# Two LN2 outputs and an exponential later on ScalarE, one Wo product later on TensorE, the sums for h earlier on VectorE

## Chip, core and metric

The kernel runs on one core of a Trainium2 chip. The metric is the device time of one launch in microseconds (us), the median of several runs. Five engines work at once, each on its own queue in program order: TensorE (PE, matmuls, with PEld for the loading of weights), VectorE (DVE), ScalarE (ACT), GpSimd (POOL) and SyncE (SP), which here only issues DMAs.

## What is computed

A transformer block on 2048 tokens of width 576: LayerNorm, attention of 32 heads of width 18 over 8 earlier positions with a step of 2, the output projection Wo and a residual, then LayerNorm, an MLP of width 4608 with a tanh gelu, and a residual.

```python
def _A_ref(x, wqkv, wo):
    ...
    W, dil = 8, 2
    qkv = (lambda x, *d: x.transpose(*d))((x @ wqkv).reshape(B, S, 3, H, Dh), 2, 0, 3, 1, 4)
    ...
    idx = pos[:, None] - off[None, :]
    ...
    logits = jnp.einsum("bhsd,bhswd->bhsw", q, kg) * scale
    logits = jnp.where(mask[None, None, :, :], logits, -1e9)
    attn = _softmax(logits, axis=-1)
    o = jnp.einsum("bhsw,bhswd->bhsd", attn, vg)
    return (lambda x, *d: x.transpose(*d))(o, 0, 2, 1, 3).reshape(B, S, D) @ wo
...
x = A_x
h = x + _A_ref(_layernorm(x, axis=-1), A_wqkv, A_wo)
h2 = h + _B_ref(_layernorm(h, axis=-1), B_w1, B_b1, B_w2, B_b2)
```

## The kernel before

The 2048 tokens are 16 tiles of 128; tile j holds tokens j, j+16, j+32 and so on, so that the 8 attended positions of a tile are whole tiles of k and v. They lie in two rings (`kv_ring`), for even and odd tiles. The order of all instructions on PE, ACT, DVE, SP and POOL is written out by hand: an instruction stands in its engine's queue where the Python code makes it.

Matmuls whose contraction is 576 deep are cut into 64-row halves that run as pairs. `phase` makes one half of a product, `visit` the first halves of two or three products ("duos"), then their second halves, each with its evacuation `evac` and with whatever `between` lists behind it. Between the two halves of a duo the rows of a PSUM bank change hands: `marker` puts a nop on POOL's queue that waits for the first half, and the second half waits for that nop. A POOL instruction that waits therefore holds back the markers queued behind it.

The QKV part has 24 visits of two duos. ACT evacuates each duo from a ring of three PSUM pairs (line 316). Lists name what follows a visit (`after`) and what stands between its evacuations (`between`). Late in this part the first two tiles already go through attention, Wo (duos added in visits 17 and 20) and LN2: `ln2` adds the residual and takes the statistics on DVE, `ln2_rstd` takes the power -0.5 on POOL (line 161), `ln2_norm` makes two ACT instructions (line 535, and the LN2 output hn at line 174), `h_tail` copies hn's last columns on POOL, and `tr_h` turns hn with matmuls into h_pt, which ACT casts to hnT (line 553), what MLP1 reads. `att_exp` is the exponential of the softmax (line 389).

After that come 8 groups of two tiles, numbered 0 to 7. Each has MLP1 (4 visits, 324 matmuls, gelu on ACT at line 580 into `h_all`) and MLP2. In these the attention of a later group runs beside it on DVE: `att_qk_a` is the product of q and k (line 346), `att_qk_add` sums over the 18 columns (line 355, four sums), `att_max`, `att_exp`, `att_den` and the product with v follow (lines 403 to 410). The next group's two Wo products (c and d; pw) stand around the start of MLP2. For each of these, `ln2_h` adds the residual on DVE (line 469), `ln2_act` takes the statistics on ACT (lines 491 to 493) and the power on POOL (line 494), and `ln2_send` writes hn and sends it through DRAM and a transposing DMA to hnT (line 510). The attention output takes the same way to oT (lines 210 and 441), which Wo reads.

Groups 0 and 1 have a plain MLP2 of 36 rows for each tile, two matmuls a row (`mlp2`, line 599); lists `ia` and `ib` say what is put ahead of which row. In group 0 the first Wo was the `late` duo: its halves stand before and after the last half of MLP1. The second stands ahead of row 19, with two rows of MLP2 as fill between its halves. Groups 2 to 7 have `mlp2_fast`, which makes MLP2 from seven products instead of eight (Strassen's scheme in Winograd's form; line 689). It needs sums and differences of blocks of `h_all` (`h_sums`, line 669, numbers 0 to 3, over 12 and then 4 or 6 of 18 block rows) and of W2 (`w2_sums`, line 659). ACT copies a partial result to a second bank as a seed (line 776). Its steps are listed by name; "hc" and "h" are what the caller hands in behind the Wo products:

```python
steps = ["wo", "hc", (1, all_), "b", "h", "e", (7, lo), (2, all_), (6, all_), "6", "7", "d", ...
```

"b" is the seed copy behind product 1; product 7 reads sum 2. "o1" and "o0" add up the output (line 720).

Of the kernel before, what the change touches and what calls it, by code (L numbers as in the profile page):

```python
# [17 lines left out]
def kernel(  # L18
# [14 lines left out]
    _, S, D = A_x.shape  # L33
# [22 lines left out]
    GROUPS = [ATT_ORDER[i:i + 2] for i in range(0, NT, 2)]  # L56
# [14 lines left out]
    x_all = wpool.tile([P, NT, D], BF16, name="x_all")  # L71
# [161 lines left out]
        tc.add_manual_dep(nop, mm_ins.name, sync_dep, reason="end of a half's visit")  # L233
        return nop

    def visit(makes, hook=None, between=(), late=None, apart=False):
        duos, marks = [], []

        def first(make):
            duos.append(make())  # L240
            marks.append(marker(phase(duos[-1], 0, None)))

        for make in makes:
            first(make)
            if hook and not isinstance(hook, dict) and len(duos) == len(makes):
                hook()
            elif isinstance(hook, dict) and len(duos) in hook:
                hook[len(duos)]()
            if apart:
                phase(duos[-1], 1, marks[-1])  # L250
                duos[-1]["evac"]()
        if apart:
            return
        for n in range(len(makes) + (late is not None)):
            if late is not None and n == len(makes) - 1:
                first(late)
            phase(duos[n], 1, marks[n])
            duos[n]["evac"]()
            for fn in (between.get(n, ()) if isinstance(between, dict) else between if n == 0 else ()):
                fn()  # L260
# [304 lines left out]
    def mlp1_duo(grp, us, tag):  # L565
        def make():
            ps = psum_pair(tag, "pm")
            ht = hnT[grp[0]]
            N = len(grp) * P
            fts = [[6 * GF * (u // 3) + 3 * GF * g + GF * (u % 3) + i for u in us for i in range(GF)] for g in range(2)]  # L570

            def op(g, i, sl, kt):
                f0 = fts[g][i] * P
                c0 = (GF * us[i // GF] + i % GF) * P
                return (w1_sb[sl, kt, f0:f0 + P] if kt < KF else w1h_sb[sl, c0:c0 + P]), ht[sl, kt, 0:N]

            def evac():
                for r in range(2):
                    for i, f in enumerate(fts[r]):
                        pace[0] = nc.scalar.activation(  # L580
                            out=hT(grp)[:, f, 0:N], in_=ps[:, r, i * N:(i + 1) * N],
                            func=ACT.Gelu_apprx_tanh, bias=b1_sb[:, f:f + 1]).ins
            return dict(g=[[ps[:, r, i * N:(i + 1) * N] for i in range(len(fts[r]))] for r in range(2)],
                        op=op, evac=evac)
        return make
# [47 lines left out]

    SR = 12
    ring1_free = [False]
    spare = [False]
    RING_T = 3 * SR * P

    def s_slot(t, m0, m1):
        if t == 2:  # L640
            return h_block(0, 1, m0, m1)
        i = (0, 1, None, 2)[t]
        if m0 < SR:
            return ring_blocks(0, (i * SR + m0) * P, m1 - m0, P)
        if not ring1_free[0]:
            rows, j = ((q_all, 15), (x_all, 10), (x_all, 8))[i] if spare[0] else (q_all, 15 - 2 * i)
            return rows[:, j, (m0 - SR) * P:(m1 - SR) * P].bitcast(F16).rearrange("p (m c) -> p m c", c=P)
        return ring_blocks(1, 6 * HALF + (i * (NM - SR) + m0 - SR) * P, m1 - m0, P)

# [51 lines left out]
    def c_(fn, *a):  # L701
        return lambda: fn(*a)
# [98 lines left out]
    with tc.manual_schedule(engines={ENG.PE, ENG.Activation, ENG.DVE, ENG.SP, ENG.Pool}):  # L801
# [132 lines left out]
        for v, fns in ((2, [(load_w1, 0)]), (3, [(load_w1, 1)]), (4, [(load_w1, 2)]), (6, [(load_wo, [0])]), (8, [(load_wo, [1, 2])]),  # L934
# [27 lines left out]
            13: [c_(att_exp, A[1])],  # L962
            16: [c_(tr_o, A[0], "D")],
            18: [c_(o_tail, A[1])],
            20: [c_(h_tail, A[0])],
            19: {0: [c_(ln2_rstd, A[0])], 1: [c_(ln2_norm, A[0])]},
            21: {0: [c_(ln2_rstd, A[1])], 1: [c_(ln2_norm, A[1])]},
            22: {0: [c_(tr_h, A[0], "D")], 1: [c_(h_tail, A[1]), c_(att_exp, A[2])]},
        }
        wo_with = {17: A[0], 20: A[1]}  # L970
        hooks = {
# [29 lines left out]
        def mlp1_plan(p, q, r, s, end):  # L1001
            return [[([2 * v + n], tag) for n, tag in enumerate(tags)] for v, tags in enumerate(((p, q), (r, s), (p, q), end))]

        def mlp1(grp, plan, ahead, between, late=None):
            for v, duos in enumerate(plan):
                call(ahead.get(v, ()))
                visit([mlp1_duo(grp, us, tag) for us, tag in duos], None, between.get(v, ()), late if v == 3 else None)

        def mlp2_tile(grp, i, tag, inserts):
            po_of[grp[i]] = psum_pair(tag, "po")  # L1010
# [14 lines left out]
        def wo_visit(*duos, fill=False):  # L1025
            visit([wo_duo(j, tag) for j, tag in duos], (lambda: [ahead[0]() for _ in range(2)]) if fill else None)

        ROWS = {6: NM, 7: NM}
        p, q, r, s = "ABDC"

        gelu_table()
        for k, g in enumerate(GROUPS):
            c, d = GROUPS[k + 1] if k + 1 < len(GROUPS) else (None, None)
            e, f = GROUPS[k + 2] if k + 2 < len(GROUPS) else (None, None)
            m1, mid, ia, ib, late_wo = {0: []}, {}, {}, {}, None
            if k in (1, 2):
                m1[0].append(c_(finish_out, GROUPS[k - 1][1]))
                m1[1], m1[3] = [c_(accumulate_hs, *g)], [c_(out_store, GROUPS[k - 1][1])]
# [5 lines left out]
            if k == 0:  # L1044
                m1[0] += [c_(halos, 1), c_(load_w2, 5), c_(att_qk_a, d), c_(att_qk_rest, d, 1), c_(halo, d, 1)]
                mid[0] = {1: [c_(exps, d)]}
                m1[1] = [c_(pv_t, c), c_(att_den, d), c_(att_pv_a, d), c_(halo, d, 2), c_(att_pv_b, d),
                         c_(dma_tr_o, d), c_(load_w2, 6), c_(add_b2, g[0]), c_(add_b2, g[1]), c_(att_qk_a, e), c_(halo, e, 1)]
                late_wo = wo_duo(c, "B")
                ia[0] = [c_(ln2_h, c), c_(ln2_act, c), c_(put_b2, c), c_(halos, 2), c_(ln2_send, c), c_(att_qk_b, e, 0)]  # L1050
                ia[19] = [lambda d=d: wo_visit((d, "A"), fill=True), c_(ln2_h, d), c_(ln2_act, d), c_(put_b2, d), c_(ln2_in, c),
                          c_(att_max, [e]), c_(att_qk_a, f), c_(ln2_send, d), c_(ln2_in, d), c_(halo, f, 1), c_(att_qk_rest, f, 1),
                          c_(exps, e, f)]
                ib[0] = [c_(finish_out, g[0]), c_(out_sum, g[0]), c_(att_den, e, f), c_(pv_sum, e), c_(send_o, e)]
                ib[8] = [c_(read_o, e)]
            elif k == 1:
                m1[0] += [c_(att_pv_sum, d), c_(send_o, d), c_(halo, d, 2)]
                m1[1] += [c_(att_qk_a, e), c_(halo, e, 1), c_(read_o, d), c_(att_qk_b, e, 0), c_(halos, 7)]
                m1[3] += [c_(out_store, GROUPS[0][0]), c_(att_qk_a, f), c_(halo, f, 1), c_(att_qk_add, f, ((0, 0, 9), (0, 0, 4)))]
                ia[0] = [c_(wo_visit, (c, "B"), (d, "C")), c_(ln2_pair, c, d), c_(att_qk_b, f, 1, 2), c_(att_max, (e, f)),  # L1060
                         c_(exps, e, f), c_(w2_sums, 0, 8, (0, 1)), c_(w2_sums, 8, 12, (0, 1)), c_(att_den, e, f)]
                ia[2] = [c_(pv_sum, e), c_(dma_tr_o, e), c_(reload_x, GROUPS[4])]
                ib[0] = [c_(finish_out, g[0]), c_(out_sum, g[0])]
            if k < 2:
                mlp1(g, mlp1_plan(p, q, r, s, (s, r, p) if k else (r, s, p)), m1, mid, late_wo)
                mlp2_tile(g, 0, "D", ia)
                mlp2_tile(g, 1, "C", ib)
                continue
            rows = ROWS.get(k, 16)
            spare[0] = k == 2  # L1070
            x = {n: [] for n in ("hc", "h", "6", "7", "in", "exp", "4", "3")}
            if 2 < k < 7:
                m1[0] += [c_(pv_sum, c), c_(send_o, c), c_(pv_sum, d), c_(read_o, c), c_(send_o, d), c_(read_o, d)]
            if k < 6:
                m1[1] = m1.get(1, []) + [c_(att_qk_one, e, 0)]
                m1.setdefault(3, [])
                if k == 2:
                    m1[0] += [c_(pv_sum, d), c_(send_o, d), c_(read_o, d)]
                    m1[3] += [c_(w2_sums, 0, 8, (2, 3)), c_(w2_sums, 8, 12, (2, 3)), c_(w2_sums, 12, 14, (0, 1)), c_(w2_sums, 14, 16, (0, 1)),
                              c_(w2_sums, 12, 14, (2, 3)), c_(w2_sums, 14, 16, (2, 3))]  # L1080
                early = (0,) if k == 5 else (0, 2)
                m1[3] += [c_(h_sums, 0, min(rows, SR), early)]
                if k == 5:
                    x["h"] += [c_(h_sums, 0, SR, (2,)), c_(h_sums, 0, SR, (1, 3))]
                else:
                    x["h"] += [c_(h_sums, 0, SR, [t for t in range(4) if t not in early])]
                x["h"] += [c_(h_sums, SR, rows)]
                x["7"] += [c_(att_max, [e]), c_(att_qk_one, f, 1), c_(att_max, [f])]
                x["exp"] += [c_(exps, e, f)]
                x["4"] += [c_(att_den, e, f)]  # L1090
            else:
                if k == 6:
                    ring1_free[0] = True
                    m1[1].append(c_(w2_sums, 16, NM))
                m1[3] = m1.get(3, []) + [c_(h_sums, 0, SR)]
                if k == 7:
                    mid[3] = {1: [c_(h_sums, SR, 16)]}
                    x["h"] += [c_(h_sums, 16, NM)]
# [56 lines left out]
```

## Time and profile before

| | us |
|---|---|
| median of 3 runs (lowest, highest) | 359.16 (359.07, 359.28) |
| the profiled execution | 359.3 |
| its span, first to last instruction | 357.5 |

Where PE starts the first MLP1 matmul of each group, from its timeline, and what the engines do until the next, from the busy times by stretch:

| stage | from | us | PE | DVE | ACT |
|---|---|---|---|---|---|
| QKV, first attention | 0 | 65.44 | 63.38 | 58.67 | 48.99 |
| group 0 | 65.44 | 38.21 | 38.20 | 36.10 | 29.21 |
| group 1 | 103.65 | 37.75 | 37.75 | 35.89 | 24.13 |
| group 2 | 141.40 | 36.18 | 35.94 | 34.82 | 24.99 |
| group 3 | 177.58 | 35.93 | 35.93 | 33.52 | 24.91 |
| group 4 | 213.51 | 35.79 | 35.79 | 33.61 | 24.91 |
| group 5 | 249.30 | 35.78 | 35.78 | 33.54 | 24.89 |
| group 6 | 285.08 | 35.54 | 35.54 | 22.66 | 19.08 |
| group 7 | 320.62 | 36.88 | 33.58 | 9.73 | 14.73 |

A row of a timeline has the start, the time from the first start to the last end of a run of like instructions, the engine, the line, the operation, the tile written and those read, shapes and the count; in brackets the idle time of the engine before it and what ended that. Matmuls overlap: each is shown for 0.27 to 0.29 us, while a new one starts every 0.06 us (64 rows, in pairs) or 0.12 us (128 rows).

### The profile page before, as it was taken

The page shows a single profiled execution, that of the slowest core. Times are in us where ns is not written, and L with a number is a line of the kernel's source. Part 1 is how long each engine was busy: PE and PEld are TensorE (multiplying, and loading weights), DVE is VectorE, ACT ScalarE, POOL GpSimd, SP SyncE. Part 2 cuts the span into 40 slices and gives each one's busy share as a digit, 9 for nine tenths or more (in the row PEclk, how much of TensorE's full clock was granted, in tenths as well). Part 3 has the DMA queues.
Part 4 walks back from the last instruction along what each step waited for, and adds up shares of the span by engine and source line. Part 5 has one row for each costly group of instructions (what it writes and reads, how often), then busy time and mean ns, then how long its engine had stood idle before and what let it go on. Part 6 is the DMA issues. An engine that isn't in the chain of part 4 may idle for free.

```text
span 357.5 us, 11586 instructions
## 1 busy us (share of the span) xinstructions
PE 351.9 (98%) x4945; PEld 291.5 (82%) x4945; DVE 298.5 (84%) x428; ACT 235.8 (66%) x524; POOL 48.4 (14%) x63
## 2 busy tenths in 40 slices
PE   8999999999999999999999999999999999999996
PEld 4777987998788877887788778877887788778874
DVE  5999999999989999999999989998999998520431
ACT  4889756996647683678566856695669566706620
POOL 2241004000212020201200220022002200210000
PEclk9999999999999999999999999999999999999999
DMA  7997799954847584732553455345535253262001
GB/s 240 332 293 169 182 255 295 388 189 87 206 72 123 162 227 76 132 72 51 100 99 85 109 108 80 89 103 112 84 88 103 62 88 51 58 130 37 4 1 34
DMA packets 63492, 46.29 MB, mean 129 GB/s; under 512 B 32192, under 2 KB 61760, under 8 KB 63440
## 3 DMA queue, kind: packets, MB, share of 16 engines
q1 hardware_dynamic: 59472, 41.50, 44.1%
q0 software_dynamic: 3744, 3.84, 9.8%
q8 instruction: 38, 0.62, 0.7%
q10 hardware_dynamic: 224, 0.22, 0.3%
q14 instruction: 14, 0.11, 0.1%
HBM read 23.38 MB, written 12.42 MB: 100 GB/s over the span
## 4 chain that ended last, share of the span: by engine, by line
PE 51%; DVE 39%; ACT 3%; issue 2%; DMA 2%; SPq 1%; POOL 0%; DVEq 0%; POOLq 0%; ACTq 0%
PE pm L222 24%; PE po L689 24%; DVE prod L355 7%; DVE prod L346 6%; DVE prod L403 6%; DVE prod L409 5%; DVE ln_stats L148 3%; PE pw L222 3%; DMA x_all<-in_A_x_dram 1%; DVE den L397 1%; DVE h L469 1%; ACT h_all L580 1%; SPq L104 1%; DVE peak L370 1%; DVE q_all L410 1%
## 5 line engine op out<-in xcount | busy, mean ns | idle before, releaser
L222 PE MATMUL pm<-hnT,w_sb 64*128 64x256 bf16 x2304 | 143.0, 269 | 0.0
L580 ACT ACTIVATE h_all<-pm,b_sb 128x256 f16<-128x256 f32 (+1 forms) x288 | 108.6, 496 | 51.0 <-PE pm L222 50.4
L222 PEld LDWEIGHTS <-w_sb 64*128 64x128 bf16 x2304 | 113.2, 94 | 13.8 <-issue 1.6
L222 PE MATMUL pq<-wq_sb,xnT 64*128 64x288 bf16 x720 | 54.9, 283 | 1.0 <-ACT kv_ring L316 0.5
L689 PEld LDWEIGHTS <-h_all 128*128 128x128 f16 x464 | 44.7, 98 | 13.4 <-issue 1.8
L222 PEld LDWEIGHTS <-xnT 64*128 64x128 bf16 x864 | 43.7, 94 | 10.4 <-issue 1.4
L355 DVE TENSOR_TENSOR prod<-prod 128x2304 bf16<-128x2304 bf16 (+1 forms) x64 | 44.2, 691 | 2.1
L403 DVE TENSOR_TENSOR prod<-kv_ring,probs 128x4608 bf16<-128x4608 bf16 x16 | 40.9, 2558 | 0.9 <-DMA kv_ring<-kv_dram 0.4
L346 DVE TENSOR_TENSOR prod<-kv_ring,q_all 128x4608 bf16<-128x4608 bf16 x16 | 40.9, 2556 | 0.8 <-POOL ln_rstd L494 0.4
L222 PE MATMUL pm<-hnT,w1h_sb 64*128 64x256 bf16 x288 | 39.5, 269 | 0.0
L409 DVE TENSOR_TENSOR prod<-prod 128x2304 bf16<-128x2304 bf16 (+1 forms) x32 | 33.9, 1058 | 1.1
L689 PE MATMUL po<-w2a_sb,h_all 128*128 128x288 bf16 (+1 forms) x252 | 34.2, 286 | 0.2 <-ACT po L776 0.2
L599 PEld LDWEIGHTS <-h_all 128*128 128x128 bf16 x288 | 27.9, 98 | 7.9 <-issue 0.9
L689 PEld LDWEIGHTS <-kv_ring 128*128 128x128 f16 x252 | 24.7, 98 | 6.2
L599 PE MATMUL po<-w2a_sb,h_all 128*128 128x288 bf16 x224 | 28.5, 286 | 0.0
L789 POOL DMA_DIRECT2D x_all<-o_sb x12 | 10.7, 890 | 125.9 <-PE pw L222 54.4
L222 PE MATMUL pq<-wqh_sb,xnT 64*128 64x288 bf16 x144 | 27.6, 283 | 0.0
L494 POOL TENSOR_TENSOR ln_rstd<-ln_var,mhalf 128x1 f32<-128x1 f32 x13 | 10.3, 795 | 78.2 <-ACT ln_var L493 78.2
L669 DVE TENSOR_TENSOR kv_ring<-h_all 128x1536 f16<-128x1536 f16 (+3 forms) x9 | 6.8, 753 | 15.9 <-ACT h_all L580 15.9
L222 PE MATMUL pw<-wo_sb,oT 64*128 64x288 bf16 x256 | 19.5, 283 | 0.0
L161 POOL TENSOR_TENSOR ln_rstd<-ln_veps,mhalf 128x1 f32<-128x1 f32 (+2 forms) x14 | 13.1, 949 | 45.8 <-DVE ln_nmean L483 28.3
L689 PE MATMUL po<-w2b_sb,h_all 128*128 128x288 bf16 (+1 forms) x112 | 18.8, 286 | 0.2 <-DVE h_all L669 0.2
(121 smaller groups left out, 410.2 us busy)
## 6 DMA issues: line engine op xcount, KB each, us to landing
w_sb<-in_B_w_dram SPq DMA_DIRECT2D x6, 768.0 KB, 6.8
kv_ring<-kv_dram SPq DMA_DIRECT2D x28, 144.0 KB, 2.4
kv_dram<-kv_ring SPq DMA_DIRECT2D x13, 288.0 KB, 3.2
w2a_sb<-in_B_w_dram SPq DMA_DIRECT2D x3, 1008.0 KB, 9.7
x_all<-in_B_b_dram SPq DMA_DIRECT2D x15, 144.0 KB, 4.3
td<-q_all SPq DMA_DIRECT2D x14, 144.0 KB, 1.8
td<-hn SPq DMA_DIRECT2D x14, 144.0 KB, 1.8
x_all<-h POOLq DMA_DIRECT2D x14, 144.0 KB, 4.8
```

The source lines that it names most:

```text
L148: nc.vector.bn_stats(out=stats[:, i, c, :], in_=src[:, c * HALF:(c + 1) * HALF])
L161: nc.gpsimd.tensor_tensor(out=rstd[:], in0=veps[:], in1=mhalf[:].to_broadcast([P, n]), op=ALU.pow)
L222: last = nc.tensor.matmul(duo["g"][r ^ swap][i], lhsT=lhsT, rhs=rhs, start=(swap == 0 and i == 0 and kt == 0), stop=(swap == 1 and kt == K ...
L346: ins = nc.vector.tensor_tensor(out=prod[:], in0=k_ring[j % 2], in1=q_all[:, j, :].unsqueeze(1) .to_broadcast([P, W, D]), op=ALU.mult).ins
L355: nc.vector.tensor_tensor(out=prod[:, :, o * H:o * H + n], in0=prod[:, :, a * H:a * H + n], in1=prod[:, :, c * H:c * H + n], op=ALU.add)
L403: nc.vector.tensor_tensor(out=prod[:].rearrange("p w (d h) -> p w d h", h=H), in0=v_ring[j % 2].rearrange("p w (d h) -> p w d h", h=H), in ...
L409: nc.vector.tensor_tensor(out=prod[:, 0:n, :], in0=prod[:, 0:n, :], in1=prod[:, n:2 * n, :], op=ALU.add)
L494: ins = nc.gpsimd.tensor_tensor(out=rstd[:], in0=var[:], in1=mhalf[:], op=ALU.pow).ins
L580: pace[0] = nc.scalar.activation(out=hT(grp)[:, f, 0:N], in_=ps[:, r, i * N:(i + 1) * N], func=ACT.Gelu_apprx_tanh, bias=b1_sb[:, f:f + 1] ...
L599: nc.tensor.matmul(banks[half], lhsT=hT(grp)[:, f, i * P:(i + 1) * P], rhs=w2_rows(f)[:, half * HALF:(half + 1) * HALF], start=(f == 0), s ...
L689: nc.tensor.matmul(bank, lhsT=l, rhs=r, start=start, stop=stop, skip_group_check=True)
L789: nc.gpsimd.dma_start(out=x_of(j), in_=o_of.pop(j), accum_op=ALU.add)
```

## The change

Five edits, and three that only tidy (a table of rows, a flag and a parameter without a use).

In the QKV part, `ln2_norm` of both tiles, `h_tail` of the first and `att_exp` of the third tile are put behind later evacuations. In group 0, the first Wo leaves MLP1's last visit and stands ahead of MLP2's row 0, with two rows as fill, and the second stands ahead of row 21 instead of 19. In group 1, the second of the four sums of a QK product stands behind both `ln2_h` instead of ahead of them. In groups 2 to 4, product sum 2 (rows 0 to 11) stands behind the first `ln2_h` and its `ln2_act` and ahead of the second, instead of ahead of both. In group 5 it stands at the same place, where it was behind both.

In the built program the number of instructions on each engine is the same, and POOL's and SP's order is unchanged apart from the markers' places.

```diff
-        for n in range(len(makes) + (late is not None)):
-            if late is not None and n == len(makes) - 1:
-                first(late)
+        for n in range(len(makes)):
             phase(duos[n], 1, marks[n])
             duos[n]["evac"]()
...
-            20: [c_(h_tail, A[0])],
-            19: {0: [c_(ln2_rstd, A[0])], 1: [c_(ln2_norm, A[0])]},
-            21: {0: [c_(ln2_rstd, A[1])], 1: [c_(ln2_norm, A[1])]},
-            22: {0: [c_(tr_h, A[0], "D")], 1: [c_(h_tail, A[1]), c_(att_exp, A[2])]},
+            19: [c_(ln2_rstd, A[0])],
+            20: {1: [c_(ln2_norm, A[0])]},
+            21: {0: [c_(h_tail, A[0]), c_(ln2_rstd, A[1])], 1: [c_(ln2_norm, A[1])]},
+            22: {0: [c_(tr_h, A[0], "D")], 1: [c_(h_tail, A[1])]},
+            23: {1: [c_(att_exp, A[2])]},
...
-                late_wo = wo_duo(c, "B")
-                ia[0] = [c_(ln2_h, c), c_(ln2_act, c), c_(put_b2, c), c_(halos, 2), c_(ln2_send, c), c_(att_qk_b, e, 0)]
-                ia[19] = [lambda d=d: wo_visit((d, "A"), fill=True), c_(ln2_h, d), c_(ln2_act, d), c_(put_b2, d), c_(ln2_in, c),
+                ia[0] = [lambda c=c: wo_visit((c, "B"), fill=True), c_(ln2_h, c), c_(ln2_act, c), c_(put_b2, c), c_(halos, 2), c_(ln2_send, c), c_(att_qk_b, e, 0)]
+                ia[21] = [lambda d=d: wo_visit((d, "A"), fill=True), c_(ln2_h, d), c_(ln2_act, d), c_(put_b2, d), c_(ln2_in, c),
...
-                m1[3] += [c_(out_store, GROUPS[0][0]), c_(att_qk_a, f), c_(halo, f, 1), c_(att_qk_add, f, ((0, 0, 9), (0, 0, 4)))]
-                ia[0] = [c_(wo_visit, (c, "B"), (d, "C")), c_(ln2_pair, c, d), c_(att_qk_b, f, 1, 2), c_(att_max, (e, f)),
+                m1[3] += [c_(out_store, GROUPS[0][0]), c_(att_qk_a, f), c_(halo, f, 1), c_(att_qk_add, f, ADDS[:1])]
+                ia[0] = [c_(wo_visit, (c, "B"), (d, "C")), c_(ln2_pair, c, d), c_(att_qk_b, f, 1, 1), c_(att_max, (e, f)),
...
-                early = (0,) if k == 5 else (0, 2)
-                m1[3] += [c_(h_sums, 0, min(rows, SR), early)]
-                if k == 5:
-                    x["h"] += [c_(h_sums, 0, SR, (2,)), c_(h_sums, 0, SR, (1, 3))]
-                else:
-                    x["h"] += [c_(h_sums, 0, SR, [t for t in range(4) if t not in early])]
-                x["h"] += [c_(h_sums, SR, rows)]
+                m1[3] += [c_(h_sums, 0, SR, (0,))]
+                x["hc"] += [c_(h_sums, 0, SR, (2,))]
+                x["h"] += [c_(h_sums, 0, SR, (1, 3)), c_(h_sums, SR, 16)]
```

More of the change, by code (lines that the diff above doesn't have):

```diff
@@ L234, in marker, with visit @@
         return nop
-    def visit(makes, hook=None, between=(), late=None, apart=False):
+    def visit(makes, hook=None, between=(), apart=False):
         duos, marks = [], []
@@ L635 @@
     ring1_free = [False]
-    spare = [False]
+    step_of = [0]
     RING_T = 3 * SR * P
@@ L645, in s_slot @@
         if not ring1_free[0]:
-            rows, j = ((q_all, 15), (x_all, 10), (x_all, 8))[i] if spare[0] else (q_all, 15 - 2 * i)
+            rows, j = ((q_all, 15), (x_all, 10), (x_all, 8))[i] if step_of[0] == 2 else (q_all, 15 - 2 * i)
             return rows[:, j, (m0 - SR) * P:(m1 - SR) * P].bitcast(F16).rearrange("p (m c) -> p m c", c=P)
@@ L1002, in mlp1_plan, with mlp1 @@
             return [[([2 * v + n], tag) for n, tag in enumerate(tags)] for v, tags in enumerate(((p, q), (r, s), (p, q), end))]
-        def mlp1(grp, plan, ahead, between, late=None):
+        def mlp1(grp, plan, ahead, between):
             for v, duos in enumerate(plan):
                 call(ahead.get(v, ()))
-                visit([mlp1_duo(grp, us, tag) for us, tag in duos], None, between.get(v, ()), late if v == 3 else None)
+                visit([mlp1_duo(grp, us, tag) for us, tag in duos], None, between.get(v, ()))
         def mlp2_tile(grp, i, tag, inserts):
@@ L1026, in wo_visit @@
             visit([wo_duo(j, tag) for j, tag in duos], (lambda: [ahead[0]() for _ in range(2)]) if fill else None)
-        ROWS = {6: NM, 7: NM}
+        FULL = (6, 7)
         p, q, r, s = "ABDC"
@@ L1034 @@
             e, f = GROUPS[k + 2] if k + 2 < len(GROUPS) else (None, None)
-            m1, mid, ia, ib, late_wo = {0: []}, {}, {}, {}, None
+            m1, mid, ia, ib = {0: []}, {}, {}, {}
             if k in (1, 2):
@@ L1064 @@
             if k < 2:
-                mlp1(g, mlp1_plan(p, q, r, s, (s, r, p) if k else (r, s, p)), m1, mid, late_wo)
+                mlp1(g, mlp1_plan(p, q, r, s, (s, r, p) if k else (r, s, p)), m1, mid)
                 mlp2_tile(g, 0, "D", ia)
@@ L1068 @@
                 continue
-            rows = ROWS.get(k, 16)
-            spare[0] = k == 2
+            rows = NM if k in FULL else 16
+            step_of[0] = k
             x = {n: [] for n in ("hc", "h", "6", "7", "in", "exp", "4", "3")}
```

## The prediction, made before the changed kernel was run

> **What bounds the kernel now.** I read four views in this order: the page's busy times, PE's timeline around every place where it starts late, the timelines of ACT, DVE and POOL at those places, and the DMA issues with their landings. The page first:
>
> ```profile
> PE 351.9 (98%) x4945; PEld 291.5 (82%) x4945; DVE 298.5 (84%) x428; ACT 235.8 (66%) x524; POOL 48.4 (14%) x63
> ```
>
> PE has 98% of the span, and the change leaves its number of matmuls alone. So an edit can only pay where PE stands still, and costs only where it makes PE wait. The idle column hides part of this: a matmul is shown for 0.28 us, yet ten of L222's 288-wide ones follow each other in 0.61 (one half of a duo starts at 58.95, the next at 59.56). I therefore compare starts. Three late starts lie where the diff works. The first two are at the end of the QKV part, on PE's timeline:
>
> ```profile
> 57.71 0.65 PE L222 MATMUL pq<-wq_sb,xnT 64*128 64x288 bf16 x8
> 58.95 0.67 PE L222 MATMUL pq<-wq_sb,xnT 64*128 64x288 bf16 x8 [0.47 <-ACT kv_ring L316]
> ...
> 64.75 0.65 PE L222 MATMUL pq<-wq_sb,xnT 64*128 64x288 bf16 x7
> 65.44 0.61 PE L222 MATMUL pm<-hnT,w_sb 64*128 64x256 bf16 x8
> ```
>
> Ten matmuls from 57.71 end their issue at 58.32, so 58.95 is 0.63 late. Eight from 64.75 take 0.49 (64.26 to 64.75 shows it), so MLP1 starts 0.20 late. ACT's timeline tells why:
>
> ```profile
> 57.17 0.29 ACT L535 ACTIVATE ln_nmean<-ln_nmean,ln_rstd 128x1 f32<-128x1 f32 x1 [1.75 <-POOL ln_rstd L161]
> 58.27 0.63 ACT L316 ACTIVATE kv_ring<-pq 128x576 bf16<-128x576 f32 x1
> ...
> 61.64 0.29 ACT L535 ACTIVATE ln_nmean<-ln_nmean,ln_rstd 128x1 f32<-128x1 f32 x1 [0.18 <-POOL ln_rstd L161]
> 62.74 0.63 ACT L316 ACTIVATE q_all<-pq 128x576 bf16<-128x576 f32 x1
> 64.39 0.43 ACT L389 ACTIVATE logits<-logits 128x256 f32<-128x256 f32 x1
> 64.69 0.70 ACT L553 CAST hnT<-h_pt 128x640 bf16<-128x640 f32 x1
> ```
>
> At 57.17 ACT has waited 1.75 for POOL's power, with the evacuation of a pq behind it (58.27); the PSUM ring of three then holds PE. At 64.39 the exponential stands ahead of the hnT cast on which MLP1 waits (64.69 + 0.70 = 65.39). The third late start is in group 2, on PE's, DVE's and ACT's timelines:
>
> ```profile
> 163.36 1.63 PE L689 MATMUL po<-w2a_sb,h_all 128*128 128x288 f16 x12
> 165.24 1.02 PE L689 MATMUL po<-w2a_sb,h_all 128*128 128x288 bf16 x7 [0.24 <-ACT po L776]
> ```
>
> ```profile
> 161.23 0.96 DVE L669 TENSOR_TENSOR h_all<-h_all 128x1536 f16<-128x1536 f16 x1
> 162.10 1.41 DVE L469 TENSOR_TENSOR h<-pw,x_all 128x576 f32<-128x576 f32 x2
> ```
>
> ```profile
> 164.79 0.39 ACT L776 COPY po<-po 128x288 f32<-128x288 f32 x1
> ```
>
> Twelve such matmuls take 1.47 (167.19 to 168.66), so product 2 was due at 164.83 and is 0.41 late. It waits for the seed copy at L776, this for h's statistics on ACT (162.88), these for h at 162.10, and h for the product sum at 161.23.
>
> **The change part by part.**
>
> *LN2 output behind evacuations (visits 19 to 21).* The 1.75 us wait goes: visit 20's two evacuations run as they come ready (their last matmuls, of 56.61 and 57.10, take 0.28, so about 56.9 and 57.45), ln_nmean follows near 58.0 with the power done since 57.14, and the 0.63 at 58.95 is gone. It doesn't all last. What is late next is the second tile's power. POOL starts it at 60.88, when DVE's ln_nmean (60.71 + 0.14) is done, and DVE runs there pass behind pass without waiting for PE. The power ends at 61.61, ACT's ln_nmean starts at 61.64 in both kernels, hn at 61.97, and the evacuation of visit 22's first duo at 62.74 ends at 63.37. Visit 23's second duo needs that bank: 63.42 at best (58.27 + 0.63 = 58.90 released PE at 58.95), against 63.51 now. So 0.09 of the 0.63 is left. POOL's queue orders the markers that let PE change halves, and h_tail and the power now stand ahead of visit 22's. Its marker came at 61.37, would come at 60.74, and is held to about 60.98 by the power's dispatch; a marker releases PE 0.07 later (POOL's record at 90.385, PE at 90.456), so 61.05, and PE wants it at 61.77 - 0.63 = 61.14. Free.
>
> *Exponential behind visit 23's evacuations.* The hnT cast moves from 64.69 to 64.39; it ends at 65.09, PE starts MLP1 at 65.14. The turned h is ready by then: its matmuls start 0.09 earlier, at 64.03, and are done 0.32 later. The two parts together give **-0.30**. The exponential goes to about 66.05; the gelu table still loads before MLP1's first gelu, which idled 0.71 at 68.72, and DVE's den of that tile is at 70.48. Bounds: 0 if another wait takes the place, -0.83 if all of it were kept.
>
> *Group 1's first Wo.* Its 18 matmuls run either way. Before, they stand between MLP1's matmuls:
>
> ```profile
> 83.74 0.67 PE L222 MATMUL pw<-wo_sb,oT 64*128 64x288 bf16 x8
> 84.34 4.83 PE L599 MATMUL po<-w2a_sb,h_all 128*128 128x288 bf16 x38
> 89.10 0.67 PE L222 MATMUL pw<-wo_sb,oT 64*128 64x288 bf16 x8
> ```
>
> Eight of these take 0.49, here 0.60 pass to the po matmul: 0.11 for the turn from 64-row to 128-row matmuls. 38 po take 38 x 0.1225 = 4.66, 4.76 pass: 0.10 for the turn back. With two rows of MLP2 as fill between its halves, the first Wo has one turn more each way: +0.21. The second Wo loses a wait: its marker stood behind the first tile's power, whose input ACT had ready at 90.24, and four po from 89.82 (0.49 + 0.10 = 90.41) became 90.46, 0.05. Two rows later it is free. Sum **+0.16**. Bounds: 0 if the turns were hidden, +0.26 if the first Wo's marker stalls too.
> The Trainium skill bears on this ("TensorEngine Tiling (Array Packing)", "Key Properties"): changing the tiling mode, not just the tile, drains TensorE. By it this edit is a loss with certainty; the trace agrees with 0.10 to 0.11 a turn, and the sum is the same by both.
> Its transfers: the first oT landed at 82.06, PE used it at 82.25 and, 0.30 earlier, would have wanted it at 81.95; in its new place it wants it at 82.82. The second landed at 88.71, wanted at about 89.5. DVE takes h of the first at 87.46 and of the second at 91.62 in both; the second's pw is now done near 91.5.
>
> *Group 1: h ahead of a QK sum.* DVE had to finish two sums (122.77, 1.37 and 0.70) before h at 124.78. pw's second half starts at 122.57, so pw is complete near 123.3 (0.70 behind, as below), and h now starts at 124.16, 0.6 earlier, and so does the chain of ACT and POOL that ends with the exponential. DVE waited for that:
>
> ```profile
> 134.33 1.04 DVE L397 TENSOR_REDUCE den<-logits 128x64 f32<-128x512 f32 x1 [0.76 <-ACT logits L389]
> ...
> 129.60 1.52 POOL L494 TENSOR_TENSOR ln_rstd<-ln_var,mhalf 128x1 f32<-128x1 f32 x1 [1.33 <-ACT ln_var L493]
> ```
>
> (The second line is POOL's.) The power's 1.52 is a DVE pass: those that start inside one end 0.40 after it (129.37 + 1.35 = 130.72, and 131.12; 54.18 + 2.55 and 57.14). Started at 129.0 it falls into the pass from 128.76 to 129.45 and ends near 129.9. DVE gains the 0.76; PE nothing here, **0**, bounds 0 and 0.
>
> *h ahead of a product sum, group 2.* h is free once pw is complete: in group 3 h started 0.70 after its second half (196.65, 197.35). That is 160.32 + 0.70 = 161.02, or 161.23 if DVE comes late. ACT's gelus end at 162.04 (157.55 + 4.49), the statistics start at 161.95 instead of 162.88, the copy at 163.86 (1.91 behind them, as now) and it is done near 164.3; PE, 0.14 ahead by the parts above, wants it at 164.69. **-0.41**. The sum now ends at 162.9 at the latest, product 7 needs it at 163.36.
>
> *The same in groups 3 and 4.* Here ACT and PE, not DVE, set h: it starts with a wait for pw at 197.35, so nothing is won and DVE idles while the sum of 0.87 slides behind h. The cover is DVE's wait at the output sums, 0.90 at 211.23 in group 3, and in group 4 0.44 at 239.28 and 0.44 at 247.01: **0**, with 0.02 to spare. Group 5's sum moves ahead of the second h; its ACT chain has 0.8 of room: 0.
>
> Sum: -0.30 + 0.16 - 0.41 = **-0.55**. The profiled execution took 359.3 (span 357.5), so 358.75; the median shown is 359.16, 0.14 below it, so **358.6**.
>
> **Rivals.**
> *The first stall is won in full.* ACT's second ln_nmean would not hold the evacuation. For it: the 0.18 at 61.64 is a short wait. Against: 61.64 is set by DVE. -0.83 + 0.16 - 0.41 = -1.08: 358.1.
> *Group 1's DVE gain is lost.* If the power doesn't get in at 129.45 it ends at 131.1 as now, den stays at 134.33, and DVE reaches group 2's output sums at 175.0 instead of 174.75. That delays group 3's second oT, which PE already awaits (landed 195.98, used at 196.03, due at 195.87). 0.26 is given back: -0.29, 358.9.
> In the Trainium skill's words ("SBUF — State Buffer", "SBUF: two separate sides") the shared port pair is "an exclusive lock", and whichever starts first holds it for its whole instruction: by that rule the power may lose again to the sum after 129.45. The trace agrees on the blocking, but the pass at 56.76 started while the power ran until 57.14.
> *Slower: DVE's lag is handed on.* In groups 3 and 4 the sum behind h makes everything after it 0.87 later on DVE. If the waits at the output sums don't absorb this, it reaches group 5's second oT, which landed at 267.48 for a matmul at 267.60: from 0.07 on every bit stops PE. Both lags: 1.74 - 0.07 - 0.55 = +1.1, 360.3; one: +0.25, 359.4. For it: the cover is as large as the lag to 0.03. Against: both waits were measured at PE's results.
>
> **How the numbers follow.** Forecast 0.44, first rival 0.16, second 0.20, third 0.20. About 0.2%, 0.7 us, is what a measurement tells from no change here. Faster than 358.44: the first rival and a quarter of the forecast's spread, 0.28. Slower than 359.88: two thirds of the third, 0.14. Between: 0.58. Range 358.0 to 359.6: it takes in the first two rivals and the third with one lag, and leaves out both lags.
>
> **What would show it.** PE: no wait near 58.3 but one near 62.9 of about 0.5; MLP1 at 65.14; po, pw, po with turns of 0.1 near 83.5; MLP1 of group 1 at 103.5; no wait on L776 near 164.7. DVE: den at 133.6, no wait at the output sums of groups 3 and 4. It is wrong if PE waits for an oT in group 5, or if 62.9 shows no wait.

## The result, and the profile after

The changed kernel took 358.67 us (median of 15 runs, 358.01 to 359.27) against 359.16 for the kernel before; that is 0.49 between the medians. The ratio as estimated from the runs is 0.9981 (95% interval 0.9973 to 0.9990), which is 0.68 us less, between 0.36 and 0.97; the ratio of the medians, 0.9986, lies within the interval. The forecast was 358.6. A second measurement, in the experiments below, gave 0.9978 (0.9967 to 0.9989). The profiled execution took 358.75, its span 357.0.

The start of each group's first MLP1 matmul on PE, and the time to the next, for two profiles of either kernel (the second of each is from the experiments). T is the start of DVE's second ln_nmean in the QKV part, the anchor of the forecast's chain:

| | before | before, 2nd | after | after, 2nd |
|---|---|---|---|---|
| T | 60.71 | 60.39 | 60.44 | 60.46 |
| start of MLP1, group 0 | 65.44 | 65.12 | 65.01 | 64.91 |
| the same from T | 4.73 | 4.73 | 4.57 | 4.45 |
| group 0 | 38.21 | 38.22 | 38.37 | 38.39 |
| group 1 | 37.74 | 37.74 | 37.74 | 37.74 |
| group 2 | 36.18 | 36.19 | 35.78 | 35.78 |
| group 3 | 35.94 | 35.78 | 36.06 | 35.84 |
| groups 4, 5, 6 | 107.11 | 107.11 | 107.10 | 107.10 |
| end of the span | 357.52 | 357.06 | 356.97 | 356.64 |

T itself differs by 0.3 between two executions of one kernel, so the stages are the better measure of the parts. They give -0.16 or -0.28 in the QKV part, +0.16 or +0.17 in group 0, -0.40 or -0.41 in group 2 and +0.12 or +0.06 in group 3. Now the lines. (A statement's line number is two lower in the changed kernel: the sum of L669 is L667, and the matmuls of L689 are L687.) The page of the changed kernel:

```profile
PE 351.1 (98%) x4945; PEld 287.4 (81%) x4945; DVE 298.2 (84%) x428; ACT 235.9 (66%) x524; POOL 47.6 (13%) x63
```

The busy times are nearly as before; only the late starts tell the two apart. The changed kernel's PE timeline around visit 21 and at MLP1 (start, time, operation, count):

```profile
58.10 0.65 PE L222 MATMUL pq<-wq_sb,xnT 64*128 64x288 bf16 x8
58.72 0.65 PE L222 MATMUL pq<-wq_sb,xnT 64*128 64x288 bf16 x8
...
64.89 0.28 PE L222 MATMUL pq<-wqh_sb,xnT 64*128 64x288 bf16 x1
65.01 0.60 PE L222 MATMUL pm<-hnT,w_sb 64*128 64x256 bf16 x8
```

Visit 21's second duo follows the first by 0.62: the late start of 0.63 is gone. MLP1 follows the last pq without a gap. ACT's timeline of the same execution:

```profile
57.33 0.65 ACT L314 ACTIVATE kv_ring<-pq 128x576 bf16<-128x576 f32 x1 [1.52 <-PE pq L222]
57.88 0.65 ACT L314 ACTIVATE q_all<-pq 128x576 bf16<-128x576 f32 x1
58.42 0.29 ACT L533 ACTIVATE ln_nmean<-ln_nmean,ln_rstd 128x1 f32<-128x1 f32 x1
...
64.23 0.69 ACT L551 CAST hnT<-h_pt 128x640 bf16<-128x640 f32 x1
```

ACT's idle time now stands before an evacuation and ends with PE, and ln_nmean waits for nothing. The first Wo in its new place, on PE:

```profile
82.69 0.66 PE L222 MATMUL pw<-wo_sb,oT 64*128 64x288 bf16 x8
83.19 0.29 PE L222 MATMUL pw<-woh_sb,oT 64*128 64x288 bf16 x2
83.40 0.66 PE L597 MATMUL po<-w2a_sb,h_all 128*128 128x288 bf16 x4
84.00 0.67 PE L222 MATMUL pw<-wo_sb,oT 64*128 64x288 bf16 x8
```

Two pw take 0.12, and 0.21 pass from 83.19 to 83.40; four po take 0.49, and 0.60 pass. Each turn costs about 0.1. Group 2, on DVE, then PE, then ACT:

```profile
160.02 0.95 DVE L667 TENSOR_TENSOR kv_ring<-h_all 128x1536 f16<-128x1536 f16 x1
160.89 0.75 DVE L467 TENSOR_TENSOR h<-pw,x_all 128x576 f32<-128x576 f32 x1
161.56 0.95 DVE L667 TENSOR_TENSOR h_all<-h_all 128x1536 f16<-128x1536 f16 x1
162.42 0.75 DVE L467 TENSOR_TENSOR h<-pw,x_all 128x576 f32<-128x576 f32 x1
```

```profile
163.09 3.35 PE L687 MATMUL po<-w2a_sb,h_all 128*128 128x288 f16 x26
```

```profile
163.58 0.39 ACT L774 COPY po<-po 128x288 f32<-128x288 f32 x1
```

h stands between the sums, the seed copy comes 1.21 earlier, and products 7 and 2 are one run of 26 matmuls without a break. What was not forecast is on DVE, 25 us ahead of den:

```profile
109.40 2.56 DVE L401 TENSOR_TENSOR prod<-kv_ring,probs 128x4608 bf16<-128x4608 bf16 x1 [0.76 <-DMA kv_ring<-kv_dram]
...
134.09 1.05 DVE L395 TENSOR_REDUCE den<-logits 128x64 f32<-128x512 f32 x1
```

den waits no more, as forecast. But DVE has lost the same 0.76 before, waiting for a halo, the row block of v that it reads back from DRAM. The kernel before shows no wait at this product (108.81). Counted from group 1's MLP1 start, den begins at 30.71, where it began at 30.68: what DVE gained at den it had lost at the halo.

### The profile page after: what moved, and what is told of

The parts are those of the page before. It is cut to its first block, busy times and chain, and to the rows that moved or that the text cites. A ratio compares the mean times of both kernels' runs of the same rounds, so it can differ in the third digit from the quotient of the medians.

```text
span 357.0 us, 11587 instructions
## 1 busy us (share of the span) xinstructions
PE 351.1 (98%) x4945; PEld 287.4 (81%) x4945; DVE 298.2 (84%) x428; ACT 235.9 (66%) x524; POOL 47.6 (13%) x63
## 4 chain that ended last, share of the span: by engine, by line
DVE 43%; PE 43%; DMA 6%; issue 3%; ACT 2%; SPq 2%; POOL 0%; DVEq 0%; POOLq 0%; ACTq 0%
PE po L687 21%; PE pm L222 19%; DVE prod L401 7%; DVE prod L353 7%; DVE prod L344 6%; DVE prod L407 5%; DVE ln_stats L148 3%; PE pw L222 2%; DMA kv_ring<-kv_dram 2%; DVE h L467 1%; DMA x_all<-in_A_x_dram 1%; DVE den L395 1%; ACT h_all L578 1%; DVE q_all L408 1%; DMA td<-q_all 1%
## 5 line engine op out<-in xcount | busy, mean ns | idle before, releaser
L222 PEld LDWEIGHTS <-w_sb 64*128 64x128 bf16 x2304 | 111.6, 94 | 15.1 <-issue 1.7
L687 PEld LDWEIGHTS <-h_all 128*128 128x128 f16 x464 | 44.8, 98 | 12.9 <-issue 1.4
L222 PEld LDWEIGHTS <-xnT 64*128 64x128 bf16 x864 | 41.9, 94 | 12.4 <-DMA xnT<-xd 0.9
L687 PE MATMUL po<-w2a_sb,h_all 128*128 128x288 bf16 (+1 forms) x252 | 34.0, 286 | 0.0
L687 PEld LDWEIGHTS <-kv_ring 128*128 128x128 f16 x252 | 24.7, 98 | 6.2
L667 DVE TENSOR_TENSOR kv_ring<-h_all 128x1536 f16<-128x1536 f16 (+3 forms) x9 | 6.8, 754 | 15.7 <-ACT h_all L578 15.7
L687 PE MATMUL po<-w2b_sb,h_all 128*128 128x288 bf16 (+1 forms) x112 | 18.8, 286 | 0.1
```

Of the source, the lines that this page charges most:

```text
L222: last = nc.tensor.matmul(duo["g"][r ^ swap][i], lhsT=lhsT, rhs=rhs, start=(swap == 0 and i == 0 and kt == 0), stop=(swap == 1 and kt == K ...
L687: nc.tensor.matmul(bank, lhsT=l, rhs=r, start=start, stop=stop, skip_group_check=True)
```

## The experiments

Ten variants of the changed kernel and one more profile of each kernel were run. All are timed against the kernel before. An interval is about 0.1% (0.36 us) to either side, so most of the times don't tell the variants from each other; the stage lengths and the late starts do.

### What the QKV part is worth

*LN2 outputs and h_tail back where they were, the exponential left behind.*

```diff
-            19: [c_(ln2_rstd, A[0])],
-            20: {1: [c_(ln2_norm, A[0])]},
-            21: {0: [c_(h_tail, A[0]), c_(ln2_rstd, A[1])], 1: [c_(ln2_norm, A[1])]},
+            20: [c_(h_tail, A[0])],
+            19: {0: [c_(ln2_rstd, A[0])], 1: [c_(ln2_norm, A[0])]},
+            21: {0: [c_(ln2_rstd, A[1])], 1: [c_(ln2_norm, A[1])]},
```

> The changed kernel with the two LN2 outputs and h_tail put back where they were; the exponential stays behind visit 23. Theory (the start of MLP1 hangs on the second tile's ln_nmean on DVE, T): PE is about 0.6 us late at visit 21's second duo again, and yet MLP1 starts about T + 4.5, at most 0.1 later than the T + 4.43 that ACT's chain allows; time 358.6 to 358.8. Rival (the stall was won in full): MLP1 starts 0.6 later than in the changed kernel, T + 5.1, time 359.2.

358.47 us, ratio 0.9985 (0.9976 to 0.9995). PE's timeline:

```profile
57.67 0.29 PE L222 MATMUL pq<-wqh_sb,xnT 64*128 64x288 bf16 x2
58.42 0.67 PE L222 MATMUL pq<-wq_sb,xnT 64*128 64x288 bf16 x8 [0.46 <-ACT kv_ring L314]
...
64.71 0.62 PE L222 MATMUL pm<-hnT,w_sb 64*128 64x256 bf16 x8
```

The late start is back in full, and MLP1 starts at 64.71 with T at 60.18: T + 4.53. The theory holds; the time is a little below the 358.6 to 358.8 expected.

*The exponential back ahead of the hnT cast, the LN2 outputs left behind.*

```diff
-            22: {0: [c_(tr_h, A[0], "D")], 1: [c_(h_tail, A[1])]},
-            23: {1: [c_(att_exp, A[2])]},
+            22: {0: [c_(tr_h, A[0], "D")], 1: [c_(h_tail, A[1]), c_(att_exp, A[2])]},
```

> The changed kernel with the exponential back ahead of the second hnT cast; the LN2 outputs stay behind the evacuations. Theory: no late start at visit 21, but PE waits elsewhere before MLP1, which starts at T + 4.73 as in the kernel before (T: end of DVE's ln_nmean start row, 60.71 there): the LN2 part alone is worth nothing; time 358.9. Rival: MLP1 starts at T + 4.1 to T + 4.3, time 358.3.

358.42 us, ratio 0.9989 (0.9979 to 0.9999). PE's timeline:

```profile
62.27 0.29 PE L222 MATMUL pq<-wqh_sb,xnT 64*128 64x288 bf16 x2
62.94 0.67 PE L222 MATMUL pq<-wq_sb,xnT 64*128 64x288 bf16 x8 [0.38 <-ACT q_all L314]
...
64.57 0.28 PE L222 MATMUL pq<-wqh_sb,xnT 64*128 64x288 bf16 x1
64.96 0.50 PE L222 MATMUL pm<-hnT,w_sb 64*128 64x256 bf16 x6
```

With T at 60.23, MLP1 starts at T + 4.73, to the digit as in the kernel before. The wait removed at visit 21 stands at visit 23 (62.27 + 0.12 = 62.39 was due, 62.94 it is), and MLP1 waits besides. The LN2 edit alone gains nothing at this point. The time missed the 358.9 expected and is nearer to the rival's 358.3; but the ratio's interval takes in a gain of 0.04 us as well as one of 0.75, and the starts speak against the rival.

*The changed kernel once more.*

> The changed kernel once more, on the same chip as the next one. Theory: without a transfer that holds PE near 42, PE is 0.56 late at visit 23's second duo near 63 and MLP1 starts 4.43 to 4.46 behind the second ln_nmean; ratio 0.998 to 0.999.

358.46 us, ratio 0.9978 (0.9967 to 0.9989). PE and ACT:

```profile
62.63 0.29 PE L222 MATMUL pq<-wqh_sb,xnT 64*128 64x288 bf16 x2
63.17 0.67 PE L222 MATMUL pq<-wq_sb,xnT 64*128 64x288 bf16 x8 [0.26 <-ACT q_all L314]
...
64.91 0.62 PE L222 MATMUL pm<-hnT,w_sb 64*128 64x256 bf16 x8
```

```profile
61.39 0.29 ACT L533 ACTIVATE ln_nmean<-ln_nmean,ln_rstd 128x1 f32<-128x1 f32 x1 [0.69 <-POOL ln_rstd L161]
...
62.49 0.63 ACT L314 ACTIVATE q_all<-pq 128x576 bf16<-128x576 f32 x1
```

Here the forecast's wait at visit 23 is seen: 0.42 late (0.56 was expected), because ACT stood 0.69 behind the second power, and MLP1 starts at T + 4.45. In the first profile PE had lost 0.8 at 42.37 to a transposing read of x (xnT) and came too late to meet it.

*One QK sum moved from ahead of the second tile's h to behind its statistics, so that T comes earlier.*

```diff
-            18: [c_(halo, A[2], 1), c_(att_qk_add, A[2], ADDS[:2])],
-            20: [c_(ln2, A[1]), c_(att_qk_rest, A[2], 0, 2)],
+            18: [c_(halo, A[2], 1), c_(att_qk_add, A[2], ADDS[:1])],
+            20: [c_(ln2, A[1]), c_(att_qk_rest, A[2], 0, 1)],
```

> The changed kernel with one sum (0.70 on DVE) of the third tile's QK product moved from ahead of the second tile's h to behind its LN2 statistics. Theory (MLP1's start hangs on DVE's second ln_nmean): counted from the first tile's ln_nmean, MLP1 starts at 10.5 to 10.7 instead of 11.05 (11.32 before the change); most of it is given back at the second oT of group 3, which hangs on DVE, so time 358.3 to 358.7. Rival (PE's own order sets it): MLP1's start doesn't move.

357.82 us (9 runs), ratio 0.9974 (0.9964 to 0.9984): the lowest time of all, though its interval overlaps that of the changed kernel. DVE's timeline:

```profile
56.53 1.36 DVE L353 TENSOR_TENSOR prod<-prod 128x2304 bf16<-128x2304 bf16 x1
57.80 0.75 DVE L467 TENSOR_TENSOR h<-pw,x_all 128x576 f32<-128x576 f32 x1
...
59.76 0.15 DVE L481 TENSOR_SCALAR ln_nmean<-ln_mv 128x1 f32<-128x1 f32 x1
```

The first ln_nmean is at 53.88, MLP1 starts at 64.47: 10.59 behind, as forecast, and the trace shows no wait of PE after 50. Counted from the first ln_nmean, the second came 0.73 sooner than in the changed kernel's second profile (5.87 for 6.60) and MLP1 0.46 sooner (10.59 for 11.05). So DVE's second ln_nmean does set the start of MLP1, up to the point where PE no longer waits. My guess that group 3 would give it back was wrong: group 3 took 35.78.

### What the Wo move costs

*The first Wo back around the last half of MLP1, the second left at row 21.*

```diff
-                ia[0] = [lambda c=c: wo_visit((c, "B"), fill=True), c_(ln2_h, c), ...
+                late_wo = wo_duo(c, "B")
+                ia[0] = [c_(ln2_h, c), ...
```

(with the `late` parameter as in the kernel before)

> The changed kernel with group 1's first Wo product back around the last half of MLP1 (no fill, no extra turns of PE); the second stays ahead of row 21. Theory: group 0 loses two turns, -0.19 to -0.21, but PE now wants the first oT 0.05 to 0.15 before it has landed; group 0 takes 38.15 to 38.35 instead of 38.38, time 358.5 to 358.7. Rival (the move was needed as cover): PE waits 0.3 or more for that oT and group 0 takes 38.5.

358.08 us, ratio 0.9978 (0.9969 to 0.9987). Group 0 takes 38.23, 0.14 to 0.16 less than in the two profiles of the changed kernel, and PE doesn't wait: it starts this Wo at 82.22, its oT landed at 82.17. The time is below the 358.5 to 358.7 expected.

*The same on top of the earlier T.*

> The changed kernel with the QK sum behind the second tile's LN2 statistics and the first Wo back around MLP1's last half. Theory (that Wo needs its oT, which hangs on DVE, 16.8 us behind MLP1's start): MLP1 starts at 10.6 behind the first ln_nmean, the oT lands at 27.7 and is wanted at 27.4, so PE waits 0.3 and group 0 takes 38.5: no better than either edit alone, 357.9 to 358.2. Rival (the two add up): no wait, group 0 takes 38.2, time 357.6.

358.24 us, ratio 0.9982 (0.9973 to 0.9991). PE:

```profile
81.97 0.66 PE L222 MATMUL pw<-wo_sb,oT 64*128 64x288 bf16 x8 [0.16 <-DMA oT<-td]
```

PE is 0.34 late there (the oT landed at 81.92), group 0 takes 38.51. So the old place costs 0.14 to 0.16 less as long as MLP1 starts late enough, and 0.12 more (38.51 against 38.39) once it starts sooner: the extra turns buy cover for a transfer.

### What h ahead of the sums is worth

*Product sum 2 of group 2 back ahead of h.*

```diff
+                if k in (2,):
+                    (x["h"] if k == 5 else m1[3]).append(c_(h_sums, 0, SR, (2,)))
+                else:
+                    x["hc"] += [c_(h_sums, 0, SR, (2,))]
-                x["hc"] += [c_(h_sums, 0, SR, (2,))]
```

> The changed kernel with product sum 2 of group 2 alone back ahead of h. Theory (two edits reach for the same stall): with the add of group 1 moved, DVE reaches the sums of group 2 up to 0.7 us sooner, h starts near 161.4 to 161.8 and product 2 is 0 to 0.3 late; time 358.7 to 358.9. Rival (this edit alone bears the gain): product 2 is 0.4 late as before, group 2 takes 36.18, time 359.05.

358.99 us, ratio 0.9997 (0.9986 to 1.0009). PE:

```profile
163.16 1.63 PE L687 MATMUL po<-w2a_sb,h_all 128*128 128x288 f16 x12
165.28 0.90 PE L687 MATMUL po<-w2a_sb,h_all 128*128 128x288 bf16 x6 [0.50 <-ACT po L774]
```

Product 2 is 0.65 late (163.16 + 1.47 = 164.63), more than in the kernel before and more than either side expected. PE is ahead by the QKV part's gain, and DVE isn't: it waited 0.98 for the halo at 109.69 and h started at 162.15, as late as ever.

*The second QK sum back ahead of group 1's h.*

```diff
-  c_(att_qk_add, f, ADDS[:1])]      ...  c_(att_qk_b, f, 1, 1)
+  c_(att_qk_add, f, ADDS[:2])]      ...  c_(att_qk_b, f, 1, 2)
```

> The changed kernel with the second sum of group 1's QK product back ahead of both h. Theory: DVE waits about 0.7 us for the exponential at den near 134 again; product 2 of group 2 is not late (group 2 takes 35.8), but DVE comes later to the output sums of group 2 and PE waits 0.3 to 0.45 for group 3's second oT instead of 0.16 to 0.27; time 358.7 to 358.9. Rival (the add bears the gain of group 2): product 2 is 0.4 late, time 359.05.

358.94 us, ratio 0.9995 (0.9983 to 1.0008). Group 2 takes 35.78 as expected and den waits 0.76 again, but PE loses the time where neither side looked, at group 2's first matmul:

```profile
141.48 0.61 PE L222 MATMUL pm<-hnT,w_sb 64*128 64x256 bf16 x8 [0.61 <-DMA hnT<-td]
```

Counted in starts it is 0.68 later than the turn to 64-row matmuls explains, and group 1 takes 38.42. The kernel before had this hnT at 141.19 for a matmul at 141.40; here DVE lost 0.78 at the halo and it landed at 141.43. With the sum behind h the same transfer is done about 3 us ahead (138.45 in the changed kernel).

*Both of these back.*

> The changed kernel with both edits to h of groups 1 and 2 back (the second QK sum ahead of group 1's h, product sum 2 ahead of group 2's h). Theory: where the halo of v lands more than 2.7 us after its issue, DVE waits for it and MLP1 of group 2 starts about as much late (0.7, as with the add alone put back); product 2 of group 2 is 0.4 late besides, less what PE has lost just before; time 359.0 to 359.5, no gain over the kernel before or little. Rival (the gain lies in the QKV part): time stays at 358.6.

359.75 us, ratio 1.0021 (1.0011 to 1.0031): slower than the kernel before, and above the 359.0 to 359.5 expected. Group 1 takes 38.41, group 2 36.72, and PE waits at both places (0.67 at 141.69, 0.86 at 166.07); DVE had lost 1.01 at the halo. The QKV part and the Wo move, with only the edits to groups 3 to 5 beside them, make the kernel slower.

*Sum 2 of groups 3, 4 and 5 back* (the same edit with `(3, 4, 5)`).

> The changed kernel with product sum 2 of groups 3, 4 and 5 back where it was; group 2 keeps the new order. Theory: nothing for PE: groups 3, 4 and 5 take 35.8 to 35.9 each; DVE's wait for h in groups 3 and 4 falls from 1.1 to 1.5 to about 0.1 to 0.5, and its waits at the output sums come back (0.9 and 0.4 + 0.4); time as the changed kernel. Rival (h ahead of the sum pays there, or its lag costs): one of these groups differs by 0.1 or more.

358.29 us, ratio 0.9985 (0.9975 to 0.9994). Groups 3, 4 and 5 take 35.78, 35.78 and 35.79. On DVE, group 3:

```profile
196.37 1.41 DVE L467 TENSOR_TENSOR h<-pw,x_all 128x576 f32<-128x576 f32 x2
...
210.19 0.95 DVE L718 TENSOR_TENSOR o_sb<-po,o_sb 128x288 f32<-128x288 f32 x2 [0.78 <-PE po L687]
```

In the changed kernel the first of these waits 1.48 for PE and the second 0.12. The wait has moved from one place to the other; PE sees neither.

### Why the halo is late

*The kernel before once more.*

> The kernel before, profiled once more. Theory (the slow halo isn't of the change's making): DVE may wait 0.5 to 1.3 for the halo of v near 109.8 here too, and then PE waits 0.4 to 0.7 for hnT at MLP1 of group 2 near 141.9. Rival: only kernels with the change show that wait, and this one shows none, group 1 takes 37.75.

359.0 us, ratio 1.0003 (0.9993 to 1.0014). No wait at the product, group 1 takes 37.74: the rival holds here, two profiles of two. What the halo's issue took to land, from the rows of its tile between 105.3 and 110.5, in this profile and in the changed kernel's first:

```profile
L341 SPq DMA_DIRECT2D kv_ring<-kv_dram x1: 320/320/320, 105.8 to 105.8; - x1
...
DMA to landing us min/median/max: 2.6/2.6/2.6
```

```profile
L339 SPq DMA_DIRECT2D kv_ring<-kv_dram x1: 320/320/320, 106.0 to 106.0; - x1
...
DMA to landing us min/median/max: 3.3/3.3/3.3
```

SyncE issues the halo as soon as DVE has done the product that reads its buffer, so it goes with DVE. POOL's two accumulating DMAs of h are queued behind a marker of MLP1's first visit, so they go with PE: 3.12 after group 1's MLP1 start in every profile, that of the last variant below apart. In the two profiles of the kernel before they came 0.65 behind the halo. In ten profiles of the changed kernel and its variants they came 0.19 to 0.51 behind it, PE having gained 0.14 or more on DVE, and the halo took 3.1 to 3.9 to land. The variant with the exponential back, where MLP1 starts as late behind T as before, had 0.54 and 2.1. The distance alone can hardly decide this: 0.51 and 0.54 are next to each other, and the nearest, 0.19, had the shortest of the long landings (3.09).

*These two DMAs issued a visit later.*

```diff
-                m1[1], ... = [c_(accumulate_hs, *g)], ...
-                m1[2] = [c_(out_sum, GROUPS[k - 1][1])]
+                m1[1], ... = [c_(accumulate_hs, *g)] if k == 2 else [], ...
+                m1[2] = [c_(accumulate_hs, *g)] * (k == 1) + [c_(out_sum, GROUPS[k - 1][1])]
```

> The changed kernel with group 1's two accumulating DMAs of h (POOL) issued behind the next MLP1 visit, about 4 us later. Theory (these DMAs slow the halo of v that lands at 109.3 in four of the six traces so far, 3.3 to 3.6 us after its issue against 2.1 to 2.6 in the others): the halo lands within 2.6 us, DVE's wait of 0.76 to 0.98 near 109.4 is gone, and group 3's second oT is awaited for 0.16 or less; time 358.2 to 358.6. Rival (the landing is chance, or other transfers do it): the wait of 0.7 or more is there again.

358.67 us, ratio 1.0005 (0.9986 to 1.0024). The halo:

```profile
DMA to landing us min/median/max: 2.1/2.1/2.1
```

DVE doesn't wait for it. Group 3 has no late oT, but it takes the same 35.78 in eight of the other nine variants. The two DMAs now run beside the store ahead of the second oT of group 1, which lands 4.84 after its issue instead of 2.22; PE is 0.23 late for that oT (121.92), and the times spread to 360.53. Moving the DMAs here wins nothing; the time is a little above the 358.2 to 358.6 expected.

Nor does it show that they delay the halo. The DMA rows from 106.9 to 107.9 (packets, MB, share of 16 engines), of the changed kernel and of this variant:

```profile
q1 hardware_dynamic: 135, 0.14, 51.0%
q8 instruction: 1, 0.02, 7.8%
```

```profile
q1 hardware_dynamic: 144, 0.15, 55.3%
```

Beside the halo's queue (q1) the changed kernel has a load of instructions, one packet of 16 KB on a queue that the profile calls instruction (q8). The times of the single packets, in all 14 profiles, go with this load. The halo is 128 packets of 1152 bytes; 120 of them have started by 1.63 to 1.82 after its issue, slow halo or not, and no packet of the accumulating DMAs starts before 1.64. In the ten profiles with the slow halo the load starts 0.84 to 1.27 after the halo's issue and takes 0.93 to 1.62; the halo's last eight packets start only when it has ended, and the halo lands 1.1 to 1.3 behind that end. In the four others, this variant among them, the load starts 1.95 to 2.10 after the issue, behind the halo's last packet.

So the accumulating DMAs don't begin the delay. They may draw out its end, where their packets run beside the last eight of the halo. That the load holds these eight back is read from the times; no run moved it alone. Why it starts 3.57 to 3.88 behind group 1's MLP1 start in the ten profiles and 4.53 to 4.57 in the four is open, and so is whether the change brings it forward.

## Why the prediction was right, and where it wasn't

**The LN2 output and the exponential, -0.30.** T + 4.73 became T + 4.45 where PE came in time, so -0.28, and the shares are as argued: without the exponential's move nothing, without the LN2 move 0.20 of it (T + 4.53). The rival that won the stall in full is out: the wait came back at visit 23 with 0.42 to 0.56 in the seven profiles where PE was in time. One sign of being wrong, "62.9 shows no wait", did come up in the first profile. There, and in the variant with sum 2 of group 2 back, PE had lost 0.8 near 42.4 and met no wait at visit 23; MLP1 started at T + 4.57 and T + 4.65. The term then is only -0.16 and -0.08: the prediction took it that nothing holds PE ahead of these visits.

**The Wo move, +0.16.** Group 0 took 0.16 and 0.17 more, and taking it back gave 0.14 to 0.16. The price was right, and so was the worth of its cover, which comes out only with an earlier MLP1.

**h ahead of group 1's QK sum.** Here a step failed: "PE nothing here, **0**, bounds 0 and 0". den's wait went as said, and the power got in behind the pass it met (129.46 to 130.45, 0.41 behind 129.35 + 0.69) while DVE's next pass, which started at 129.96, already ran. But I worked out DVE's gain on an unchanged DVE. I had not asked what else could hold DVE ahead of den: the halo came late, and DVE lost 0.53 to 1.35 there in all profiles of the changed kernel and its variants but two, the one with the exponential back and the one with the two DMAs moved. The late halo goes with the load of instructions; what brings that forward stays open. The edit then was no spare: without it PE loses 0.68 at group 2. My margin for that hnT was a comparison of 141.19 with 141.40, and I took it for enough. Of the power, the Trainium skill ("SBUF — State Buffer", "SBUF: two separate sides") says that whichever of VectorE and GpSimd starts first keeps the port pair that they share for its whole instruction. That the power ended only behind the pass agrees; that the next pass began 0.49 ahead of the power's end does not, as far as POOL's rough spans can tell.

**h ahead of product sum 2 in group 2, -0.41.** -0.40 and -0.41. In the changed kernel it carries more than its own term: without it product 2 is 0.65 late.

**Groups 3 to 5, 0.** As said, to 0.01 in groups 4 and 5, with DVE's idle time moved from the output sums to h. The third rival, a lag handed to group 5's oT, didn't come.

**The second rival** came in part and by another cause: DVE's gain of group 1 was lost to the halo, not to the power. Group 3 took 0.12 and 0.06 more, of the 0.26 worked out. That this is the lost gain is not shown: the two profiles of the kernel before differ by 0.16 there, and four variants with the slow halo and no wait of PE in groups 1 and 2 took 35.78.

The sum of the measured stages, with the second pair of profiles, is -0.28 + 0.17 - 0.41 + 0.06 = -0.46, against -0.55 forecast; with the first pair it is -0.16 + 0.16 - 0.40 + 0.12 = -0.28. The medians differ by 0.49. That 358.6 met 358.67 to 0.07 is in part luck: T alone differs by 0.3 between two executions.

## What to carry to other kernels

When a transfer is late, look at its packets and at all that moves beside them, loads of instructions too, before blaming the transfer that was issued next to it; an experiment that ends the delay shows its cause only if nothing else moved with it. An edit that gains little by itself can be the cover without which another one loses; take both back before calling either free. And a wait removed in a chain counts only up to the next event that is fixed by another engine: find that event first, and count from it.

## What was not expected of the hardware

A DMA of 144 KB on SyncE's queue, the halo of group 1, landed 2.1 to 2.6 us after its issue in four profiles and 3.1 to 3.9 us in ten. In the ten, and only there, a 16 KB load of instructions started 0.84 to 1.27 us after that issue and took 0.93 to 1.62 us, and the last eight of the DMA's 128 packets started only behind it. The other 120 had started within 1.82 us of the issue, against 1.71 us in the four. What sets the time of the load was not tested.
